# Two small projections moved onto one accumulator bank, their conversions reserved on VectorE, and score groups that carry a VectorE tile sent ahead

## The chip, the cores and the metric

The kernel runs on one core of one Trainium2 chip. The metric is the device time of one execution in microseconds, taken as the median of several runs.

## The reference

One transformer layer on 2048 rows of width 448. `h = x + Attention(LN(x))`, with 16 query heads of width 28 that share one key and one value head, and then `h2 = h + B(LN(h))`, where B adds a gated MLP for the 8 rows with the highest router score alone. Cut to what matters here:

```python
q = (x @ wq).reshape(B, S, H, Dh).transpose(0, 2, 1, 3); k = x @ wk; v = x @ wv
p = softmax(einsum("bhqd,bkd->bhqk", q, k) * Dh ** -0.5)
o = einsum("bhqk,bkd->bhqd", p, v)          # 16 heads, one K and one V
h = x + o.transpose(0, 2, 1, 3).reshape(B, S, H * Dh) @ wo
n = layernorm(h); r = n @ w_r; idx = argsort(-r)[:8]
h2 = h + n + scatter_add(idx, (silu(n[idx] @ w_gate) * (n[idx] @ w_up)) @ w_down * sigmoid(r[idx]))
```

Nearly all of the time goes into the 2048 x 2048 x 16 scores and their exponentials.

## The kernel before

**Blocks and slots.** The work goes over 16 blocks b of 128 query rows. A block has 64 score tiles: 16 groups of 128 keys by four lanes of 32 partitions, a lane holding four heads. A tile is 128 keys by 512 (four heads by 128 queries) and fills one of the eight PSUM banks. From block 1 on 16 of the 64 tiles go to VectorE and 48 to ScalarE. ScalarE's 48 are dealt into 17 slots, numbered 0 to 16: three tiles in most slots, two in the three slots that the tuple `TWO` names. A slot is one group of score matmuls on TensorE (`act_unit`, "a score group") and one exponential on ScalarE over its two or three banks (L760, the tile P).

**VectorE's tiles.** In every slot but the third of `TWO` (slot 11) the score group carries one matmul more, into the bank `VB`, for VectorE. `dve_tile` converts it to an integer form of the exponential (L785, the tile Y), which frees `VB` for the next score group. After every fourth tile `dve_batch` makes three shifted copies: two on VectorE (L794), one on GpSimd (L796). They are not started while the other engine holds the port that the planner models as shared (`port=True`). P and Y are multiplied with V on TensorE, four matmuls at a time (`pv_group`), all accumulating in the bank `ACC`. VectorE's tiles of a block begin four slots before the block (`LEAD`).

**Banks.** Score groups alternate between two halves, banks 0 to 2 in one slot and 3 to 5 in the next. A slot with two tiles leaves the third bank of its half free, and that bank is lent to a small projection ("misc"): in slot 2 the output projection of two blocks earlier (`out_proj`, four matmuls, then the residual sum `hbuf` on VectorE, L655), in slot 5 the query projection for two blocks later (`q_project`, 16 matmuls, then the conversion to `Q` on VectorE, L549). `misc(b, k)` gives the bank: 2 or 5, by whether the slot is even or odd. So the projections of slots 2 and 5 sit in different halves. The next score group of that half that has three tiles writes the lent bank, and so waits until the projection's result has been converted.

**The order on the engines.** Every engine runs its instructions in a fixed order. A planner in the kernel's Python (`_Graph.plan`) makes it beforehand from assumed durations. Three of its rules matter here:

- TensorE (`pe_choice`): score groups have `hold=AC`. Each has a last moment, a fixed lead before ScalarE comes free. Other work, P·V matmuls and projections, is put ahead of a score group if it ends before that moment.
- VectorE (`dve_choice`): operations marked `urgent` are reserved for. An operation that isn't urgent starts only if it ends within 150 ns of the moment at which the next urgent one becomes ready. Only the conversions of score tiles (`dve_tile`) are urgent.
- `fill` puts matmuls on zeros into TensorE's idle time.

`close_acc` copies a finished block's `ACC` to `Ot` (L805), and P·V matmuls of the next block wait for it. `post_block` divides it by the row sums by way of DRAM and GpSimd. After `hbuf` follow the statistics of the second layer norm (L657 to L671), the router's product `junk` (L690) and `r_col` (L693) on VectorE, and the two scaled copies on GpSimd (L682, L685).

Of the kernel before, what the change touches and what calls it, by code (L numbers as in the profile page):

```python
# [24 lines left out]
class _Graph:  # L25
# [5 lines left out]
    WINDOW = 3413.0  # L31
    FLOOR = 0.5
    SLIP = 150.0

    def __init__(self, sems, dma_sems, after=None):
        self.after = after
# [9 lines left out]
    def op(self, eng, fns, dur, reads=(), writes=(), prio=None, dma=False, name="", mode=None, pos=(0, 1, 2, 3),  # L46
           hold=None, deps=(), port=False, urgent=False, blk=None, kb=0):
        o = _Op()
        o.eng, o.dur, o.dma, o.name = eng, float(dur), dma, name
        o.mode, o.pos, o.hold, o.port, o.urgent, o.blk, o.kb = mode, pos, hold, port, urgent, blk, kb  # L50
        o.fns = list(fns) if isinstance(fns, (list, tuple)) else [fns]
        o.lat = 2700.0 if dma else self.LAT[eng]
        o.prio = 0.0 if self.after else (self.prio if prio is None else prio)
        o.idx = len(self.ops)
        o.deps = {}
        o.sig = False

        def need(p, sem):
            if p is not None and p is not o:
                o.deps[p.idx] = o.deps.get(p.idx, False) or sem  # L60

        for p in deps:
            need(p, not (p.eng == eng == PE) or p.dma)
        for k in reads:
            for p in self.last_w.get(k, ()):
                need(p, not (p.eng == eng == PE) or p.dma)
            if isinstance(k, tuple) and k[0] == "ps":
                for p in self.readers.get(k, ()):
                    if p.eng != eng:
                        need(p, True)  # L70
        for k in writes:
            for p in self.last_w.get(k, ()):
                need(p, (p.eng != eng) or (eng != PE) or p.dma)
            for p in self.readers.get(k, ()):
                need(p, p.eng != eng or p.dma or dma)
        if self.after and eng == PO and not dma:
            need(self.last_pool, True)
            self.last_pool = o
        for k in reads:
            self.readers.setdefault(k, []).append(o)  # L80
        for k in writes:
            self.last_w[k] = [o]
            self.readers[k] = []
        self.ops.append(o)
        return o
# [6 lines left out]
    def pe_choice(self, lst, free):  # L92
        t = free[PE]
        cand = [(self.pe_start(o, max(t, o.ready)), o) for o in lst]
        m = min(s for s, o in cand) + 1.0
        held = [(s, o, max(o.ready, free[o.hold] - self.LEAD_IN - 40.0)) for s, o in cand if o.hold]
        lim = min([l for s, o, l in held], default=1e12)
        now = [(o.prio, o.idx, s, o) for s, o, l in held if s <= m]
        if not now:
            now = [(o.prio, o.idx, s, o) for s, o in cand  # L100
                   if not o.hold and s <= m and s + o.dur + self.SWITCH <= lim + 1.0]
        if not now:
            p = min((s, o.prio, o.idx, o) for s, o, l in held if l <= lim + 1.0)
            return p[0], p[3]
        p = min(now)
        return p[2], p[3]
# [212 lines left out]
def _main(nc, G, sb, ps, psb, flag, scr, A_x, A_wq, A_wk, A_wv, A_wo, B_w_r, B_w_gate, B_w_up, B_w_down, out,  # L319
# [224 lines left out]
    def q_project(b, bank):  # L544
        pieces([mm(ps[:, bank, g * 128:(g + 1) * 128], wq_pad[0:CK, ch, g, :], xnT[0:CK, ch, b * 128:(b + 1) * 128],
                   ch == 0, ch == NCH - 1) for g in range(4) for ch in range(NCH)], 4, 56,
               reads=["wq_pad", ("xnT", b)], writes=[pk(bank)])
        q = b % NQ
        G.op(DV, lambda e: e.tensor_scalar(Q[:, q, :, :].rearrange("p g n -> p (g n)"), ps[:, bank, :], qone[:, 0:1],  # L549
                                           None, ALU.add), dvt(512),  # L550
             reads=[pk(bank), "qone"], writes=[("Q", q)], prio=G.prio - 900)

    GROUPS = [[0], [1], [2, 3], [4, 5], [6, 7], [8, 9], [10, 11], [12, 13], [14, 15]]

# [95 lines left out]
    def out_proj(b, bank):  # L650
        t, rb, hr = b, b % 2, b % 3
        tail = b == NB - 1
        pieces([mm(ps[:, bank, 0:D], On[:, rb, g * 128:(g + 1) * 128], wo_pad[:, g, :], g == 0, g == 3)
                for g in range(4)], 1, 189, reads=[("On", rb, 0), ("On", rb, 1), "wo_pad"], writes=[pk(bank)])
        G.op(DV, lambda e: e.tensor_tensor(hbuf[:, hr, :], ps[:, bank, 0:D], x_sb[:, t, :], ALU.add), dvt(D),  # L655
             reads=[pk(bank), ("x", t)], writes=[("h", hr)], prio=G.prio - 900)
        G.op(DV, lambda e: e.bn_stats(bn6[:, t, :], hbuf[:, hr, :]), dvt(D), reads=[("h", hr)], writes=[("bn6", t)])  # L657
        G.op(DV, lambda e: e.bn_aggr(mv[:, t, :], bn6[:, t, :]), 110, reads=[("bn6", t)], writes=[("mv", t)])
        G.op(DV, lambda e: e.tensor_scalar(st[:, t, 7:8], mv[:, t, 1:2], EPS, None, ALU.add), 70,
             reads=[("mv", t)], writes=[("st7", t)])  # L660
        if tail:
            G.op(AC, lambda e: e.activation(st[:, t, 7:8], st[:, t, 7:8], ACT.Ln), 200,
                 reads=[("st7", t)], writes=[("st7", t)])
            G.op(AC, lambda e: e.activation(st[:, t, 4:5], st[:, t, 7:8], ACT.Exp, scale=-0.5), 200,
                 reads=[("st7", t)], writes=[("st4", t)])
        else:
            G.op(PO, lambda e: e.tensor_tensor(st[:, t, 4:5], st[:, t, 7:8], nhalf[:, 0:1], ALU.pow), 600,
                 reads=[("st7", t), "nhalf"], writes=[("st4", t)])
        G.op(DV, lambda e: e.tensor_scalar(st[:, t, 5:6], st[:, t, 4:5], 1.0, None, ALU.add), 70,
             reads=[("st4", t)], writes=[("st5", t)])  # L670
        G.op(DV, lambda e: e.scalar_tensor_tensor(st[:, t, 6:7], mv[:, t, 0:1], -1.0, st[:, t, 4:5],  # L671
                                                  ALU.mult, ALU.mult), 80,
             reads=[("mv", t), ("st4", t)], writes=[("st6", t)])
        if tail:
            G.op(AC, lambda e: e.activation(xn[:, t, :], hbuf[:, hr, :], ACT.Identity, bias=st[:, t, 6:7],
                                            scale=st[:, t, 4:5]), 560,
                 reads=[("h", hr), ("st4", t), ("st6", t)], writes=[("xn", t)])
            G.op(AC, lambda e: e.activation(outf[:, t, :], hbuf[:, hr, :], ACT.Identity, bias=st[:, t, 6:7],
                                            scale=st[:, t, 5:6]), 560,
                 reads=[("h", hr), ("st5", t), ("st6", t)], writes=[("outf", t), ("x", t)])  # L680
        else:
            G.op(PO, lambda e: e.tensor_scalar(outf[:, t, :], hbuf[:, hr, :], st[:, t, 5:6], st[:, t, 6:7],  # L682
                                               ALU.mult, ALU.add), 800,
                 reads=[("h", hr), ("st5", t), ("st6", t)], writes=[("outf", t), ("x", t)])
            G.op(PO, lambda e: e.tensor_scalar(xn[:, t, :], hbuf[:, hr, :], st[:, t, 4:5], st[:, t, 6:7],  # L685
                                               ALU.mult, ALU.add), 800,
                 reads=[("h", hr), ("st4", t), ("st6", t)], writes=[("xn", t)])
        if not tail:
            evs.append(dma(out_v[:, t, :], outf[:, t, :], [("out", t)], reads=[("outf", t)], prio=G.prio + 30))
        G.op(DV, lambda e: e.scalar_tensor_tensor(junk[:, :], hbuf[:, hr, :], st[:, t, 4:5], w_rb[:, :],  # L690
                                                  ALU.mult, ALU.mult, accum_out=st[:, t, 2:3]), 700,
             reads=[("h", hr), ("st4", t), "w_rb"], writes=["junk", ("st2", t)], port=True)
        G.op(DV, lambda e: e.scalar_tensor_tensor(r_col[:, t:t + 1], st[:, t, 6:7], sw[:, 0:1], st[:, t, 2:3],  # L693
                                                  ALU.mult, ALU.add), 80,
             reads=[("st6", t), "sw", ("st2", t)], writes=[("r", t)], port=True)

    NVB = [0] + [4] * (NB - 1)
    LEAD = 4
    TWO = (2, 5, 11)
    TWO_LAST = (2, 7, 11)  # L700
    LAG = 4
    slots = []
# [43 lines left out]
    def act_unit(n):  # L746
# [7 lines left out]
        if v:  # L754
# [1 line left out]
            reads += [("Q", v[0] % NQ), ("K", v[1])]  # L756
            writes.append(pk(VB))
            pos.append(vi)
        sops.append(G.op(PE, fns, 216, mode="S", pos=pos, hold=AC, reads=reads, writes=writes, prio=t - 30))
        G.op(AC, lambda e: e.activation(P[:, s0:s0 + w, :], ps[:, b0:b0 + w, :], ACT.Exp,  # L760
                                        bias=-(ZERO + SHIFT) * OCT, scale=OCT), w * 427 + 50,
             reads=[pk(b0 + k) for k in range(w)], writes=[("P", s0 + k) for k in range(w)], prio=t - 30)
# [205 lines left out]
    t = NT - 1  # L968
# [182 lines left out]
```

## Time and profile before

| | |
|---|---|
| median of 3 runs | 438.6 us (437.02 to 438.82) |
| the profiled execution | 440.31 us, span 438.4 us |
| TensorE busy | 343.5 us (78%) |
| VectorE busy | 337.7 us (77%) |
| ScalarE busy | 371.7 us (85%), of which 358.7 us are the 281 exponentials of L760 |
| GpSimd busy | 186.1 us (42%) |
| mean granted TensorE clock | 0.986; 1.00 from block 1 to block 15, half in one stretch of some 10 us after the last block |

No engine is full: the busiest has 15% of the span idle. Two warnings for the reading. A matmul's end is modelled, so TensorE's busy share is no measure of how full it is. And an exponential that follows another overlaps its predecessor's end, so that the time lost between two is read from the distance of their ends and not from the idle time alone.

### The profile page before, as it was taken

To read this page: it belongs to the slowest core of one execution; us is meant where nothing else is said; L and a number is where in the kernel's file an instruction comes from. 1 tells how busy PE (TensorE), PEld (TensorE's weight loads), DVE (VectorE), ACT (ScalarE), POOL (GpSimd) and SP (SyncE) were. 2 spreads that over 40 slices of the span, in tenths; PEclk is the share of its full clock that TensorE was granted. 3 is DMA by queue.
4 is the path that set the end of the run, shared out by engine and by line. 5 is a ranking of instruction groups with operands and counts; after the bars stand their busy time and mean duration, and the time that the engine had idled before them with its cause. 6 is when DMAs were issued, how large, how long until landed. Compare 5 with 4: busy or idle time off the path is not lost.

```text
span 438.4 us, 9042 instructions
## 1 busy us (share of the span) xinstructions
PE 343.5 (78%) x3718; PEld 131.1 (30%) x3718; DVE 337.7 (77%) x708; ACT 371.7 (85%) x311; POOL 186.1 (42%) x200
## 2 busy tenths in 40 slices
PE   3899777877777778778787777787878777786994
PEld 2445321312222322222232222222223221222673
DVE  6965686979797978888897978787979787976333
ACT  4768799999989899999999998989898989995130
POOL 5332134362536363544535363635454545363001
PEclk9999999999999999999999999999999999999599
DMA  8991000010101010101000000000010101000000
GB/s 211 216 243 29 0 4 26 3 37 2 37 3 37 2 37 2 38 2 35 2 26 14 16 22 9 32 4 34 4 37 3 37 3 37 3 12 12 1 2 20
DMA packets 15782, 14.18 MB, mean 32 GB/s; under 512 B 6061, under 2 KB 12981, under 8 KB 15733
## 3 DMA queue, kind: packets, MB, share of 16 engines
q1 hardware_dynamic: 15701, 13.51, 11.5%
q8 instruction: 32, 0.52, 0.5%
q14 instruction: 17, 0.14, 0.1%
q0 software_dynamic: 32, 0.01, 0.0%
HBM read 11.42 MB, written 2.09 MB: 31 GB/s over the span
## 4 chain that ended last, share of the span: by engine, by line
DVE 46%; PE 34%; ACT 13%; issue 4%; DMA 1%; POOL 0%; SPq 0%; POOLq 0%
PE ps L436 33%; DVE Y L785 24%; ACT P L760 13%; DVE Y L794 8%; DVE Ot L805 2%; DVE Q L549 2%; PE ps L439 2%; DVE junk L690 2%; DVE bn L657 2%; DVE hbuf L655 2%; DVE r_col L693 2%; DMA wq_sb<-in_A_wq_dram 1%; DVE xnT L594 1%; DVE K L604 1%; DVE Y L1016 0%
## 5 line engine op out<-in xcount | busy, mean ns | idle before, releaser
L760 ACT ACTIVATE P<-ps 128x1536 bf16<-128x1536 f32 (+2 forms) x281 | 358.7, 1405 | 31.8 <-PE ps L436 29.3
L785 DVE TENSOR_SCALAR Y<-ps 128x512 int16<-128x512 f32 x240 | 165.1, 688 | 58.2 <-PE ps L436 58.1
L796 POOL TENSOR_TENSOR Y<-Y,step 128x1024 int32<-128x1024 int32 x60 | 113.4, 1890 | 149.3 <-DVE Y L794 90.3
L436 PE MATMUL ps<-Q,K 32*128 32x512 bf16 x1024 | 113.3, 389 | 61.2 <-DVE Y L785 44.7
L436 PE MATMUL ps<-Y,Vs 128*32 128x512 bf16 x960 | 86.8, 385 | 16.6 <-DVE Ot L805 11.3
L794 DVE TENSOR_SCALAR Y<-Y 128x2048 int16<-128x2048 int16 x120 | 82.1, 684 | 0.1
L436 PEld LDWEIGHTS ps<-Q,K 32*128 32x128 bf16 x1024 | 33.1, 91 | 159.8 <-ACT P L760 128.0
L436 PE MATMUL ps<-P,Vs 128*32 128x512 bf16 x784 | 76.2, 392 | 0.3 <-ACT P L760 0.3
L436 PEld LDWEIGHTS ps<-Y,Vs 128*32 128x32 bf16 x960 | 22.1, 93 | 59.1 <-issue 19.6
L436 PE MATMUL ps<-zero 128*32 128x512 bf16 x115 | 34.9, 386 | 0.0
L682 POOL TENSOR_SCALAR x_sb<-hbuf,st 128x448 bf16<-128x448 f32 x15 | 15.1, 1005 | 33.5 <-DVE st L671 33.5
L436 PEld LDWEIGHTS ps<-P,Vs 128*32 128x32 bf16 x784 | 18.9, 93 | 33.5 <-issue 30.1
L641 POOL TENSOR_TENSOR On<-Ot,Rb 128x256 bf16<-128x256 f32 x30 | 21.2, 724 | 1.5 <-DMA Rb<-l_scr 1.5
L436 PE MATMUL ps<-xnT,wq_pad 112*128 112x128 bf16 x256 | 20.9, 232 | 0.6 <-DVE mv L562 0.6
L617 POOL TENSOR_SCALAR Vs<-Vf 128x64 bf16<-128x64 f32 (+1 forms) x36 | 8.9, 248 | 24.9 <-DVE Vf L614 23.2
L436 PEld LDWEIGHTS ps<-xnT,wq_pad 112*128 112x128 bf16 x256 | 15.8, 103 | 7.6 <-issue 7.5
L1041 POOL DMA_INDIRECT out_dram<-Y,idxu x1 | 1.1, 1116 | 35.7 <-issue 35.7
L436 PE MATMUL ps<-wo_pad,On 128*128 128x448 bf16 x64 | 15.7, 363 | 0.4 <-POOL On L641 0.4
L549 DVE TENSOR_SCALAR Q<-ps,qone 128x512 bf16<-128x512 f32 x16 | 11.9, 743 | 3.3 <-PE ps L436 3.3
L439 PE MATMUL ps<-ident,xn 128*112 128x128 bf16 x68 | 8.5, 291 | 6.3 <-DVE xn L572 6.3
L436 PEld LDWEIGHTS ps<-zero 128*32 128x32 bf16 x115 | 10.9, 97 | 7.9 <-issue 1.3
L690 DVE SCALAR_TENSOR_TENSOR junk<-hbuf,st,w_rb 128x448 f32<-128x448 f32 x16 | 11.7, 733 | 0.0
(159 smaller groups left out, 226.9 us busy)
## 6 DMA issues: line engine op xcount, KB each, us to landing
Rb<-l_scr SPq DMA_DIRECT2D x14, 256.0 KB
out_dram<-x_sb SPq DMA_DIRECT2D x15, 112.0 KB, 1.7
wg_sb<-in_B_w_gate_dram SPq DMA_DIRECT2D x1, 1568.0 KB, 15.0
wu_sb<-in_B_w_up_dram SPq DMA_DIRECT2D x1, 1568.0 KB, 21.7
wd_sb<-in_B_w_down_dram SPq DMA_DIRECT2D x1, 1568.0 KB, 25.1
x_sb<-in_A_x_dram SPq DMA_DIRECT2D x3, 448.0 KB, 5.7
wq_sb<-in_A_wq_dram SPq DMA_DIRECT2D x2, 196.0 KB, 3.0
wo_pad<-in_A_wo_dram SPq DMA_DIRECT2D x4, 98.0 KB
```

Source lines behind the costliest of these rows:

```text
L436: return lambda e: e.matmul(o, lhsT=l, rhs=r, start=start, stop=stop)
L439: return lambda e: e.transpose(o, i, ident[0:p, 0:p])
L549: G.op(DV, lambda e: e.tensor_scalar(Q[:, q, :, :].rearrange("p g n -> p (g n)"), ps[:, bank, :], qone[:, 0:1], None, ALU.add), dvt(512), ...
L617: G.op(PO, lambda e, v=v: e.tensor_scalar(Vs[:, v, t0:t0 + n, :], Vf[:, t0:t0 + n, :], VC[v], 1.0, ALU.mult, ALU.mult), 150 + 32 * n * 1.5 ...
L641: G.op(PO, lambda e, c=c: e.tensor_tensor(On[:, rb, c], Ot[:, rb, c], Rb[:, rb, c], ALU.mult), 750, reads=[("Ot", rb), ("Rb", rb)], writes ...
L655: G.op(DV, lambda e: e.tensor_tensor(hbuf[:, hr, :], ps[:, bank, 0:D], x_sb[:, t, :], ALU.add), dvt(D), reads=[pk(bank), ("x", t)], writes ...
L682: G.op(PO, lambda e: e.tensor_scalar(outf[:, t, :], hbuf[:, hr, :], st[:, t, 5:6], st[:, t, 6:7], ALU.mult, ALU.add), 800, reads=[("h", hr ...
L690: G.op(DV, lambda e: e.scalar_tensor_tensor(junk[:, :], hbuf[:, hr, :], st[:, t, 4:5], w_rb[:, :], ALU.mult, ALU.mult, accum_out=st[:, t, ...
L760: G.op(AC, lambda e: e.activation(P[:, s0:s0 + w, :], ps[:, b0:b0 + w, :], ACT.Exp, bias=-(ZERO + SHIFT) * OCT, scale=OCT), w * 427 + 50, ...
L785: G.op(DV, lambda e: e.tensor_scalar(Y[:, y, 0, q, :].bitcast(I16), ps[:, VB, :], 0.0, 32639.0 - STEP[3], ALU.max, ALU.min), dvt(512), rea ...
L794: done = [G.op(DV, lambda e, c=c: e.tensor_single_scalar(y[c].bitcast(I16), y[0].bitcast(I16), STEP[c], ALU.add), 600, reads=r, writes=[(" ...
L796: G.op(PO, lambda e: e.tensor_tensor(y[3].bitcast(I32), y[0].bitcast(I32), step3[:, 0:1].broadcast_to([128, 1024]), ALU.add), 2050, reads= ...
```

## The change

- The second entry of `TWO` goes from 5 to 4: the slots with two tiles are 2, 4 and 11. Slots 2 and 4 are of one half, so both projections use the same bank, one after the other, and slot 4's score group doesn't write it. The next score group that does is that of slot 6. The query projection is queued one slot earlier. The last block keeps its own tuple `TWO_LAST`, (2, 7, 11).
- The conversions `Q` (from block 3 on) and `hbuf` become urgent in the planner.
- A score group that carries a VectorE tile is urgent for `pe_choice`: its last moment is at most 100 ns (`EARLY`) after it is ready.
- A GpSimd operation that writes what an earlier GpSimd operation read now waits for it by a semaphore.

```diff
+    EARLY = 100.0
...
             for p in self.readers.get(k, ()):
-                need(p, p.eng != eng or p.dma or dma)
+                need(p, p.eng != eng or p.dma or dma or eng == PO)
...
-        held = [(s, o, max(o.ready, free[o.hold] - self.LEAD_IN - 40.0)) for s, o in cand if o.hold]
+        held = [(s, o, max(o.ready, min(free[o.hold] - self.LEAD_IN - 40.0, o.ready + self.EARLY
+                                        if o.urgent else 1e12))) for s, o in cand if o.hold]
...
         # q_project: the conversion to Q
-             reads=[pk(bank), "qone"], writes=[("Q", q)], prio=G.prio - 900)
+             reads=[pk(bank), "qone"], writes=[("Q", q)], prio=G.prio - 900, urgent=b > 2)
...
         # out_proj: hbuf
-             reads=[pk(bank), ("x", t)], writes=[("h", hr)], prio=G.prio - 900)
+             reads=[pk(bank), ("x", t)], writes=[("h", hr)], prio=G.prio - 900, urgent=True)
...
-    TWO = (2, 5, 11)
+    TWO = (2, 4, 11)
...
-        sops.append(G.op(PE, fns, 216, mode="S", pos=pos, hold=AC, reads=reads, writes=writes, prio=t - 30))
+        sops.append(G.op(PE, fns, 216, mode="S", pos=pos, hold=AC, reads=reads, writes=writes, prio=t - 30,
+                         urgent=bool(v)))
```

## Rows read from the trace of the kernel before

**Rows 1.** Busy times by stretch: length; PE, PEld, DVE, ACT, POOL; PEclk; DMA share, GB/s

```profile
106.64:336.92 230.28, 183.01 (x2030) 60.39 (x2030) 193.37 (x361) 218.73 (x171) 111.94 (x90) 1.00 0.06 19
```

**Rows 2.** Who waited for whom: us in total, times, longest

```profile
ACT P L760 <- PE ps L436: 29.3, 32, 3.0
...
PE ps L436 <- DVE hbuf L655: 2.9, 13, 0.2
```

**Rows 3.** Chain that ended last: start, us, what; conversion to Q

```profile
106.64 0.66 DVE Q L549
...
336.92 0.66 DVE Q L549
```

**Rows 4.** Timeline of ScalarE, slots 1 to 6 and 13: start, us, instruction

```profile
191.89 2.48 ACT L760 ACTIVATE P<-ps 128x1536 bf16<-128x1536 f32 x2
...
194.45 1.45 ACT L760 ACTIVATE P<-ps 128x1536 bf16<-128x1536 f32 x1
...
196.86 1.45 ACT L760 ACTIVATE P<-ps 128x1536 bf16<-128x1536 f32 x1 [0.96 <-PE ps L436]
...
198.21 1.02 ACT L760 ACTIVATE P<-ps 128x1024 bf16<-128x1024 f32 x1
...
199.34 1.45 ACT L760 ACTIVATE P<-ps 128x1536 bf16<-128x1536 f32 x1
...
208.25 1.52 ACT L760 ACTIVATE P<-ps 128x1536 bf16<-128x1536 f32 x1
```

**Rows 5.** Timeline of TensorE, slots 2 to 4, and slot 12

```profile
192.49 0.39 PE L436 MATMUL ps<-Q,K 32*128 32x512 bf16 x3
192.81 0.93 PE L436 MATMUL ps<-wo_pad,On 128*128 128x448 bf16 x4
193.67 0.40 PE L436 MATMUL ps<-Y,Vs 128*32 128x512 bf16 x4
194.00 0.40 PE L436 MATMUL ps<-Q,K 32*128 32x512 bf16 x4
...
196.42 0.40 PE L436 MATMUL ps<-Q,K 32*128 32x512 bf16 x4 [0.22 <-DVE hbuf L655]
196.75 0.84 PE L436 MATMUL ps<-xnT,wq_pad 112*128 112x128 bf16 x12
...
206.22 0.40 PE L436 MATMUL ps<-Q,K 32*128 32x512 bf16 x4
```

**Rows 6.** Timeline of VectorE, slots 2 to 5

```profile
192.93 0.69 DVE L785 TENSOR_SCALAR Y<-ps 128x512 int16<-128x512 f32 x1
193.53 0.68 DVE L794 TENSOR_SCALAR Y<-Y 128x2048 int16<-128x2048 int16 x1
194.45 0.69 DVE L785 TENSOR_SCALAR Y<-ps 128x512 int16<-128x512 f32 x1 [0.23 <-PE ps L436]
195.06 0.68 DVE L805 COPY Ot<-ps 128x512 f32<-128x512 f32 x1
195.66 0.61 DVE L655 TENSOR_TENSOR hbuf<-ps,x_sb 128x448 f32<-128x448 f32 x1
```

**Rows 7.** Timeline of VectorE, slots 11 to 14

```profile
205.79 0.68 DVE L690 SCALAR_TENSOR_TENSOR junk<-hbuf,st,w_rb 128x448 f32<-128x448 f32 x1
...
206.51 0.55 DVE L693 SCALAR_TENSOR_TENSOR r_col<-st,sw 128x1 f32<-128x1 f32 x1
206.98 0.68 DVE L785 TENSOR_SCALAR Y<-ps 128x512 int16<-128x512 f32 x1
208.25 0.69 DVE L785 TENSOR_SCALAR Y<-ps 128x512 int16<-128x512 f32 x1 [0.59 <-PE ps L436]
209.54 0.69 DVE L785 TENSOR_SCALAR Y<-ps 128x512 int16<-128x512 f32 x1 [0.59 <-PE ps L436]
```

**Rows 8.** Groups of the page: busy, mean ns, idle before

```profile
L794 DVE TENSOR_SCALAR Y<-Y 128x2048 int16<-128x2048 int16 x120 | 82.1, 684 | 0.1
```

**Rows 9.** Timeline of VectorE, block 15, while GpSimd ran L682 and L685

```profile
388.31 0.85 DVE L794 TENSOR_SCALAR Y<-Y 128x2048 int16<-128x2048 int16 x1
```

## The prediction

> **What bounds the kernel now.** I read the waits first. ScalarE's exponentials wait for TensorE 29.3 us in all [rows 2]; that is the largest idle time of the busiest engine, so I looked for where in a block it lies. The chain that ended last shows the conversion to Q at the same place of each block: from 106.64 to 336.92 are ten blocks [rows 3], 23.03 us each. In that stretch the granted clock is 1.00 and no engine is full (ScalarE 218.7 of 230.3 us) [rows 1], so it is a matter of waits.
>
> A block's floor on ScalarE comes from distances of ends (start plus length). The two-bank exponential of slot 5 ends 0.92 after its predecessor (198.31 to 199.23) [rows 4]. Slot 6's ends at 200.79 and slot 13's at 208.25 + 1.52 = 209.77 [rows 4]; of these 8.98 us slot 11 has 0.92, and the six over three banks 1.343 each. 14 x 1.343 + 3 x 0.92 = 21.56. The block takes 23.03: 1.47 us are lost in each. The ends of slots 2, 3, 4, 5 and 6 are 194.37, 195.90, 198.31, 199.23, 200.79 [rows 4]: slot 3 loses 1.53 - 1.34 = 0.19, slot 4 1.07, slot 6 0.22, together 1.48.
>
> Slot 4's cause stands in its row: the score group at 196.42 waited for `hbuf` [rows 5], because slot 4 writes the bank that the output projection borrowed in slot 2. The projection's matmuls had ended at 193.74 [rows 5], but VectorE took an L794 copy at 193.53, then Y, then Ot, and `hbuf` only at 195.66 to 196.27 [rows 6]. The waits name `hbuf` 13 times [rows 2]: blocks 3 to 15 each have this stall. (The 0.2 us given there is only TensorE's idle time; what the end of the exponential lost is 1.07.) Slot 3's cause: the VB bank came free at 193.62, when Y ended [rows 6], but TensorE put a Y·V group at 193.67 ahead, and the scores went at 194.00 [rows 5]. Slot 6 is the step behind the late slot 4.
>
> There is a second loop with hardly any slack, through the single VB bank: score matmuls, Y, next score matmuls. Where nothing disturbs it Y follows Y after 1.285 us (208.25 to 209.54) [rows 7], of which 0.45 are from scores to Y (194.00 to 194.45) [rows 5, 6]. ScalarE needs 1.343 for three banks, but 0.92 in a two-bank slot, so around slots 2 to 5 the VB loop is the slower one.
>
> A sum over both checks this. From the scores of slot 12 to those of slot 4 are nine steps of the loop, 11.57; the late Y of slot 12 adds 0.31 (below), slot 3 0.23 and slot 4 1.13 (1.51 and 2.42 between the scores [rows 5], less 1.285). From slot 4's scores to the end of its exponential 1.89 (196.42 to 198.31), then 0.92, 1.56 and four times 1.343 to slot 10's end, which is 200.79 + 5.37 = 206.16, and 0.06 from there to slot 12's scores at 206.22 [rows 5]: 9.80. Together 23.04, against 23.03.
>
> **The change, part by part.** *Slot 4 no longer writes the lent bank.* Its wait for `hbuf` goes whatever VectorE does: -1.07, and with it -0.22 in slot 6. *Urgent score groups*: the Y·V group goes behind slot 3's scores: -0.19. That alone, if all else stayed, would be 13 x 0.19 = 2.5 us. P·V groups slide back behind the scores. TensorE has room for them: a group of four holds it for 0.33 (193.67 to 194.00) [rows 5], and a block's 17 score groups and 28 P·V groups make 14.9, with some 1.8 for the two projections 16.7 of 23.
>
> With all of it gone the block would be at ScalarE's 21.56. What the VB loop then allows: slot 12's scores to slot 5's are ten steps, 12.85; from there ScalarE leads again: 0.45 + 1.45 for slot 5's exponential (three banks now), five of 1.343 to slot 10's end, 0.06 to slot 12's scores: 8.68. Together 21.53. So the two loops are all but level, and every delay of a Y between slots 12 and 5 lengthens the block, less 0.03. The delays:
>
> *`hbuf` reserved on VectorE.* It becomes ready in the middle of a loop step: the projection ends 1.25 after slot 2's scores began (192.49 to 193.74) [rows 5], `hbuf` can start at about 1.30 and takes 0.61 [rows 6], until 1.91. The Y of slot 3 would be due at 1.285 + 0.45 = 1.735. It is 0.18 late. The L794 copy that stood at 193.53 is refused there and moves to a later gap: the VectorE has 230.3 - 193.4 = 36.9 us idle in ten blocks [rows 1], 3.7 a block, and the gaps in front of Y are 0.59 [rows 7], each large enough for one. Bounds: 0 if it falls into a gap, 0.61 if Y waits for all of it.
>
> *The Q conversion reserved.* Its matmuls need `hbuf` done (1.91) and take about 0.9 (estimated from 0.84 for twelve, end included [rows 5]); some go before slot 4's scores, some behind. Its turn then comes after slot 4's Y, in a gap that it fills (0.66 [rows 3] against 0.675, the loop's 1.285 less 0.61 of Y from 194.45 to 195.06 [rows 6]). Cost 0; bounds 0 and 0.66.
>
> *`junk` and `r_col`.* They stay, 205.79 to 206.98 = 1.19 us [rows 7]; slot 12's Y, due 0.45 after the scores at 206.22 [rows 5], came at 206.98: 0.31 late. They follow `hbuf`, so their place moves; I keep 0.31. Bounds 0 and 0.52 (1.19 less a gap of 0.675).
>
> *Semaphore waits on GpSimd.* Operations that rewrite what GpSimd read occur in the setup alone; in a block its writes go to tiles that other engines read. GpSimd is busy 111.9 of 230.3 us [rows 1], which hides them: 0, and if a hit came in a block, one wait of a few tenths off the path.
>
> Sum: 0.18 + 0 + 0.31 = 0.49 of delay, less 0.03 of slack: the block takes 21.56 + 0.46 = 22.02, 1.01 less than 23.03. Thirteen blocks have the stall: 13.1 us. The profiled execution (440.31, span 438.4) is 1.7 above the median; from it this gives 427.2, from the median 425.5. I predict 426. In general, with d the delay per block, the time is 438.6 - 13 x (1.50 - d), and not below 438.6 - 13 x 1.47 = 419.5.
>
> **The rivals.** *ScalarE sets the pace (d under 0.3: 420 to 423).* For it: old gaps of 0.59 stand empty. Against: `hbuf` and the router's operations have lengths that don't fit the gap.
>
> *The conversions cost Y whole turns (d 0.8 to 1.33: 429 to 436).* If Q's last matmuls fall behind slot 5's scores, its conversion comes after slot 5's Y and ends at 0.45 + 0.61 + 0.66 + 0.1 = 1.82 after those scores; slot 6, the next that writes the shared bank, was due at 1.285: +0.54, d = 1.03, 432.5. For it: the matmuls can't start before 1.91, and slot 4's scores, due at 2 x 1.285 + 0.18 = 2.75, now go ahead of what is left of them. Against: what is left then has a whole step before slot 5's.
>
> *No measurable change (d 1.33 to 1.67).* The same wait in slot 6, and `hbuf` holding slot 3's Y for its full 0.61 instead of 0.18: d = 1.03 + 0.43 = 1.46, 438.1. The stall of slot 4 would have become one of slot 6.
>
> *Slower: VectorE and GpSimd collide.* The planner lays L794 and GpSimd's work apart by assumed durations; in a denser block the real ones overlap. In block 15 an L794 copy under GpSimd's scaling took 0.85 [rows 9] against a mean of 0.684 over all 120 [rows 8]: +0.17. With d = 0.49 it takes (1.67 - 0.49) / 0.17, seven of a block's eight copies, to be slower by over 0.5%; all eight give d = 1.85, 443. Against it: the mean of 0.684 says that nearly none collides now. The Trainium skill (GPSIMD Engine Reference, section Key points) states that GpSimd shares its SBUF interfaces with VectorE and contends with VectorE instructions in a two-port mode; the trace agrees with this 0.85, and by that rule every overlap would be paid, which is what this rival assumes.
>
> **How the numbers follow.** About 0.5%, 2.2 us, can be told from no change. Forecast (d 0.3 to 0.8, 423 to 429.5) 0.45; ScalarE's pace 0.15; whole turns 0.20; no change 0.10; slower 0.10. Faster is 0.45 + 0.15 + 0.20 = 0.80. For 8 in 10 the range goes from 420 (next to nothing lies under the floor) to 437, which leaves out the slower case and most of the no-change one.
>
> **What would show it.** Right: the distance from one Q conversion to its match a block later is near 22.0; slot 4's scores wait for Y and not for `hbuf`; slot 3's scores start when Y ends; `hbuf` stands directly ahead of slot 3's Y; no exponential of slots 3 to 6 ends over 0.5 late. Wrong: slot 6's scores wait for Q (second and third rival), or L794's mean length is well above 0.684 (fourth), or the order that the planner makes differs from block to block. The prediction falls if the planner, whose assumed loop differs from the measured 1.285, packs more than one operation into VectorE's gaps of 0.675.

## The result and the profile after

The changed kernel takes 426.81 us (median of 4 runs, 422.86 to 430.47) against 438.71 us (437.02 to 440.9): a ratio of 0.970, interval 0.960 to 0.979. Executions over 1.5% longer than the fastest of their kernel count in the medians of this document and not in the ratios, so that the two need not match. The profiled execution took 428.56 us, its span is 426.8 us.

First the page of the changed kernel, and its busy times in one stretch in which both of its longer blocks lie (columns as in [rows 1]):

```profile
PE 339.0 (79%) x3709; PEld 129.4 (30%) x3709; DVE 342.9 (80%) x708; ACT 370.2 (87%) x311; POOL 195.6 (46%) x200
...
L797 DVE TENSOR_SCALAR Y<-Y 128x2048 int16<-128x2048 int16 x120 | 85.3, 712 | 0.1
```

```profile
95.00:314.00 219.00, 176.59 (x2006) 58.25 (x2006) 195.34 (x358) 215.60 (x169) 116.57 (x90) 1.00 0.06 20
```

The busy times hardly change and the waits do. The waits of the changed kernel, as in [rows 2]:

```profile
ACT P L763 <- PE ps L438: 17.7, 31, 3.0
...
PEld ps L438 <- DVE hbuf L657: 5.8, 13, 0.7
```

ScalarE's wait for TensorE falls from 29.3 to 17.7 us. `hbuf` is still waited for 13 times, but now by the query projection's first weights, which want its bank, and no longer by scores.

Now one block (block 7, slots 2 to 6) on TensorE, to be laid beside [rows 5]:

```profile
184.16 0.39 PE L438 MATMUL ps<-Q,K 32*128 32x512 bf16 x3
184.48 0.93 PE L438 MATMUL ps<-wo_pad,On 128*128 128x448 bf16 x4
185.43 0.40 PE L438 MATMUL ps<-Q,K 32*128 32x512 bf16 x4
185.76 0.62 PE L438 MATMUL ps<-P,Vs 128*32 128x512 bf16 x8
186.31 0.40 PE L438 MATMUL ps<-xnT,wq_pad 112*128 112x128 bf16 x4
186.82 0.39 PE L438 MATMUL ps<-Q,K 32*128 32x512 bf16 x3
187.15 0.84 PE L438 MATMUL ps<-xnT,wq_pad 112*128 112x128 bf16 x12
188.09 0.40 PE L438 MATMUL ps<-Q,K 32*128 32x512 bf16 x4
...
189.52 0.40 PE L438 MATMUL ps<-Q,K 32*128 32x512 bf16 x4 [0.27 <-DVE Y L788]
```

and on VectorE, beside [rows 6] (the last row is the next block's conversion to Q):

```profile
184.59 0.69 DVE L788 TENSOR_SCALAR Y<-ps 128x512 int16<-128x512 f32 x1
185.45 0.62 DVE L657 TENSOR_TENSOR hbuf<-ps,x_sb 128x448 f32<-128x448 f32 x1 [0.17 <-PE ps L438]
185.99 0.68 DVE L788 TENSOR_SCALAR Y<-ps 128x512 int16<-128x512 f32 x1
186.59 0.68 DVE L808 COPY Ot<-ps 128x512 f32<-128x512 f32 x1
187.26 0.69 DVE L788 TENSOR_SCALAR Y<-ps 128x512 int16<-128x512 f32 x1
188.03 0.75 DVE L551 TENSOR_SCALAR Q<-ps,qone 128x512 bf16<-128x512 f32 x1
188.70 0.68 DVE L788 TENSOR_SCALAR Y<-ps 128x512 int16<-128x512 f32 x1
...
209.96 0.75 DVE L551 TENSOR_SCALAR Q<-ps,qone 128x512 bf16<-128x512 f32 x1
```

Slot 3's scores follow the projection at once (185.43) with no Y·V group between. `hbuf` stands directly ahead of slot 3's Y, which was due at 185.43 + 0.45 = 185.88 and starts at 185.99. Slot 4's scores, at 186.82, wait for nothing but the Y that ended at 186.67. The distance from one Q conversion to the next is 209.96 - 188.03 = 21.93 us, against 23.03 in [rows 3].

The end of each exponential gives what is left per regular block: 0.29 us in slot 5 and 0.09 in slot 6, instead of 0.19, 1.07 and 0.22 in slots 3, 4 and 6. Blocks 9 and 12 are longer: 22.96 us. In block 9 a VectorE row of slot 1 is out of line, and GpSimd's rows beside it say why. VectorE:

```profile
226.51 1.79 DVE L797 TENSOR_SCALAR Y<-Y 128x2048 int16<-128x2048 int16 x1
```

GpSimd:

```profile
223.94 1.97 POOL L643 TENSOR_TENSOR On<-Ot,Rb 128x256 bf16<-128x256 f32 x2 [1.28 <-DMA Rb<-l_scr]
225.86 1.89 POOL L799 TENSOR_TENSOR Y<-Y,step 128x1024 int32<-128x1024 int32 x1
```

The broadcast `Rb` landed late, `On` waited 1.28 us for it, the copy on GpSimd came later than planned and ran until 227.75, and VectorE's copy, which should take 0.68, ended 0.55 after that. That is the collision that the fourth rival was made of. Ahead of block 12, the other long one, `On` waited again, and nowhere else in the blocks did it wait over 0.1 us. GpSimd:

```profile
291.03 1.70 POOL L643 TENSOR_TENSOR On<-Ot,Rb 128x256 bf16<-128x256 f32 x2 [1.54 <-DMA Rb<-l_scr]
```

### The profile page after: what moved, and what is told of

Same layout as the page of the kernel before. It is cut to its first block, busy times and chain, and to the rows that moved or that the text cites. A ratio compares the mean times of both kernels' runs of the same rounds, so it can differ in the third digit from the quotient of the medians.

```text
span 426.8 us, 9032 instructions
## 1 busy us (share of the span) xinstructions
PE 339.0 (79%) x3709; PEld 129.4 (30%) x3709; DVE 342.9 (80%) x708; ACT 370.2 (87%) x311; POOL 195.6 (46%) x200
## 4 chain that ended last, share of the span: by engine, by line
PE 42%; DVE 30%; ACT 21%; issue 5%; DMA 1%; POOL 0%; SPq 0%; POOLq 0%
PE ps L438 40%; ACT P L763 21%; DVE Y L788 15%; DVE Y L797 4%; DVE Q L551 2%; DVE junk L692 2%; PE ps L441 1%; DVE r_col L695 1%; DVE xnT L596 1%; DVE K L606 1%; DMA wq_sb<-in_A_wq_dram 1%; DVE Ot L808 0%; DVE Y L1019 0%; DVE hbuf L657 0%; DVE mv L660 0%
## 5 line engine op out<-in xcount | busy, mean ns | idle before, releaser
L763 ACT ACTIVATE P<-ps 128x1536 bf16<-128x1536 f32 (+2 forms) x281 | 357.4, 1416 | 17.8 <-PE ps L438 17.7
L788 DVE TENSOR_SCALAR Y<-ps 128x512 int16<-128x512 f32 x240 | 165.5, 689 | 38.0 <-PE ps L438 37.2
L438 PE MATMUL ps<-Y,Vs 128*32 128x512 bf16 x960 | 84.4, 383 | 5.1 <-DVE Y L797 2.4
L438 PEld LDWEIGHTS ps<-Q,K 32*128 32x128 bf16 x1024 | 34.3, 91 | 170.3 <-ACT P L763 135.4
L797 DVE TENSOR_SCALAR Y<-Y 128x2048 int16<-128x2048 int16 x120 | 85.3, 712 | 0.1
L438 PE MATMUL ps<-P,Vs 128*32 128x512 bf16 x784 | 75.2, 388 | 0.1
L438 PEld LDWEIGHTS ps<-Y,Vs 128*32 128x32 bf16 x960 | 22.2, 94 | 35.5 <-issue 16.3
L643 POOL TENSOR_TENSOR On<-Ot,Rb 128x256 bf16<-128x256 f32 x30 | 22.9, 784 | 2.9 <-DMA Rb<-l_scr 2.8
L687 POOL TENSOR_SCALAR xn<-hbuf,st 128x448 bf16<-128x448 f32 x15 | 17.4, 1158 | 0.0
L657 DVE TENSOR_TENSOR hbuf<-ps,x_sb 128x448 f32<-128x448 f32 x16 | 10.0, 624 | 4.3 <-PE ps L438 4.3
L441 PE MATMUL ps<-ident,xn 128*112 128x128 bf16 x68 | 7.6, 269 | 6.4 <-DVE xn L574 6.4
```

What stands on the lines that cost most here:

```text
L438: return lambda e: e.matmul(o, lhsT=l, rhs=r, start=start, stop=stop)
L441: return lambda e: e.transpose(o, i, ident[0:p, 0:p])
L643: G.op(PO, lambda e, c=c: e.tensor_tensor(On[:, rb, c], Ot[:, rb, c], Rb[:, rb, c], ALU.mult), 750, reads=[("Ot", rb), ("Rb", rb)], writes ...
L788: G.op(DV, lambda e: e.tensor_scalar(Y[:, y, 0, q, :].bitcast(I16), ps[:, VB, :], 0.0, 32639.0 - STEP[3], ALU.max, ALU.min), dvt(512), rea ...
L797: done = [G.op(DV, lambda e, c=c: e.tensor_single_scalar(y[c].bitcast(I16), y[0].bitcast(I16), STEP[c], ALU.add), 600, reads=r, writes=[(" ...
```

## The experiments

A block's length below is the distance between the ends of exponentials. Every ratio is to the kernel before on the same chip.

**The parts one by one.** The tuple alone, in the kernel before:

```diff
-    TWO = (2, 5, 11)
+    TWO = (2, 4, 11)
```

> The kernel before with the tuple of two-bank slots changed to (2, 4, 11) and nothing else. My theory (a block takes 21.53 us plus the delay of score tiles between slots 12 and 5): slot 4 no longer waits for hbuf, but hbuf is still converted late (after the L794 copy, Y and Ot, about 3.8 us behind slot 2's scores), so the query projection starts late on the same bank and slot 6 waits for Q instead: a block of 22.6 to 23.0 us, 433 to 438 us in all. Rival, that moving the slot alone removes the stall: 22.0 us a block, 426 us.

437.6 us, ratio 0.995 (0.991 to 0.999). Blocks alternate, 24.29 and 21.73 us. Nearly the whole difference is one stall of 2.33 us in slot 6 of every second block. TensorE and then VectorE in block 5:

```profile
146.68 1.07 PE L436 MATMUL ps<-xnT,wq_pad 112*128 112x128 bf16 x16
149.04 0.40 PE L436 MATMUL ps<-Q,K 32*128 32x512 bf16 x4 [1.30 <-DVE mv L658]
```

```profile
145.14 0.61 DVE L655 TENSOR_TENSOR hbuf<-ps,x_sb 128x448 f32<-128x448 f32 x1
145.82 0.69 DVE L785 TENSOR_SCALAR Y<-ps 128x512 int16<-128x512 f32 x1
146.43 1.28 DVE L794 TENSOR_SCALAR Y<-Y 128x2048 int16<-128x2048 int16 x2
147.63 0.62 DVE L657 BATCH_NORM_STATS2 bn<-hbuf 128x6 f32<-128x448 f32 x1
148.16 0.73 DVE L549 TENSOR_SCALAR Q<-ps,qone 128x512 bf16<-128x512 f32 x1
```

The conversion to Q ends at 148.89 and slot 6's scores follow at 149.04. (The row names the statistics, which end at 148.98; what these scores need is the bank that Q's conversion frees.) As expected, the stall of slot 4 has become one of slot 6.

The early score groups alone:

```diff
+        held = ... min(free[o.hold] - self.LEAD_IN - 40.0, o.ready + self.EARLY if o.urgent else 1e12) ...
+        sops.append(G.op(PE, fns, 216, mode="S", ..., urgent=bool(v)))
```

> Of the change only the early score groups: the two-bank slots are (2, 5, 11) and no conversion is reserved. As I priced it: slot 3's 0.19 us per block comes back, hbuf stays late, slot 4 still waits: 22.8 us a block, 436 us. Rival, after the run without the early groups cost 28 us more than the changed kernel: they are worth much by themselves, 430 us or less.

434.06 us, ratio 0.986 (0.978 to 0.993). Slot 3's loss is gone as expected, but slot 4's falls too, from 1.07 to between 0.36 and 0.96: blocks of 22.13 to 22.73 us. The expectation (22.8, 436) was too small a gain, the rival (430) too large.

The reservation alone:

```diff
-             ... writes=[("Q", q)], prio=G.prio - 900)
+             ... writes=[("Q", q)], prio=G.prio - 900, urgent=b > 2)
-             ... writes=[("h", hr)], prio=G.prio - 900)
+             ... writes=[("h", hr)], prio=G.prio - 900, urgent=True)
```

> Of the change only the reservation of the Q and hbuf conversions. Loop theory: hbuf ends 1.9 us behind slot 2's scores, slot 4 doesn't wait: 22.2 us a block, 428 us. Rival, that a score group queued behind a Y.V group waits with it for GpSimd's copy, as in the run without the early groups: one such stall of 2.5 us in most blocks, 24 us a block, over 445 us.

439.93 us, ratio 0.999 (0.995 to 1.003). Neither the 428 us of the loop theory nor the rival's 445 came. Again there are two sorts of block: 22.20, as the loop theory had it, and 23.77. The long ones have an L794 copy of 1.80 us in slot 1, under GpSimd's copy (165.76 to 167.65):

```profile
166.40 1.80 DVE L794 TENSOR_SCALAR Y<-Y 128x2048 int16<-128x2048 int16 x1
```

**The parts taken away one by one.** Without the early groups (`urgent=bool(v)` removed):

> The changed kernel without the early score groups (none marked urgent). My theory: slot 3's scores go behind a Y.V group again, 0.2 us per block back: 22.1 us a block, 13 x 0.2 = 2.6 us more than the changed kernel. Rival, that the score order is what brings the gain: 22.6 us a block or more, over 434 us.

455.22 us, ratio 1.036 (1.030 to 1.041); 24.14 us a block, 2.58 of loss in slot 5 (block 14 takes 29.67, with 6.87 lost in that slot). My expectation of 22.1 is far off. VectorE in block 6:

```profile
168.87 1.28 DVE L796 TENSOR_SCALAR Y<-Y 128x2048 int16<-128x2048 int16 x2
170.31 0.75 DVE L551 TENSOR_SCALAR Q<-ps,qone 128x512 bf16<-128x512 f32 x1 [0.15 <-PE ps L438]
170.98 0.62 DVE L659 BATCH_NORM_STATS2 bn<-hbuf 128x6 f32<-128x448 f32 x1
...
171.94 0.69 DVE L787 TENSOR_SCALAR Y<-ps 128x512 int16<-128x512 f32 x1
```

Slot 4's scores are at 169.10 there, so its Y was due at 169.55; it is placed behind two copies, Q and the statistics, and in the program it waits for GpSimd, whose copy ends at 171.91. The copies have been put so far back that one of the three Y buffers isn't free. The rival's number is nearer, but not its mechanism: it is VectorE's tile that waits, and the score group behind it.

Without the reservation (both `urgent` flags of the conversions removed):

> The changed kernel without the reservation of the Q and hbuf conversions on VectorE. My theory: hbuf waits behind a copy again and slot 6 waits for Q: 22.4 to 22.8 us a block, 431 to 436 us. Rival, that the reservation is worth nothing once both projections share the bank: 21.9 us a block, 427 us.

442.59 us, ratio 1.006 (1.002 to 1.011): blocks of 24.15 and 22.17 in turn, with the same 2.33 us in slot 6 as with the tuple alone. The theory names the right place; the size was 0.5 us a block too small.

With the slots at (2, 5, 11) and all the rest:

> The changed kernel with the two-bank slots back at (2, 5, 11). My theory: with hbuf reserved it is done 1.9 us behind slot 2's scores, and slot 4's are due at 2.57, so slot 4 doesn't wait even where it writes the lent bank: 22.0 us a block, 426 to 428 us, the same as the changed kernel; the move of the slot is worth next to nothing. Rival, that the shared bank is what removes the stall: 22.8 us or more a block, over 435 us.

465.5 us, ratio 1.058 (1.050 to 1.065); blocks 2 to 13 take 22.2 to 26.2 us and block 15 32.3. I had expected no difference. From block 5 to block 13 slot 13 loses 1.36, and the granted clock falls to half in the blocks. A stretch of that and what stands at slot 13 of block 8, VectorE and then GpSimd:

```profile
213.50:223.00 9.50, 8.85 (x56) 1.77 (x57) 5.67 (x12) 8.30 (x7) 3.31 (x3) 0.50 0.04 13
```

```profile
236.37 1.85 DVE L673 SCALAR_TENSOR_TENSOR st<-mv,st 128x1 f32<-128x1 f32 x1
238.14 0.68 DVE L788 TENSOR_SCALAR Y<-ps 128x512 int16<-128x512 f32 x1
```

```profile
236.30 1.89 POOL L799 TENSOR_TENSOR Y<-Y,step 128x1024 int32<-128x1024 int32 x1
```

`st6` (L673), one number per partition, takes 1.85 us in place of 0.15: it starts 0.07 after GpSimd's copy and ends with it. Y and with it the scores stand behind it. The planner does not count this operation as a user of the shared port.

**Is it the collision?** First by telling the planner (`port=True` on that operation):

> The changed kernel with the slots back at (2, 5, 11), as in the run of 465.5 us, but with the small product st6 (L673, two SBUF inputs, 1.84 us instead of 0.15 under GpSimd's copy) entered in the planner as a user of the shared port. Theory that the collision makes that run slow: the stall of 1.36 us in slot 13 is gone, the granted clock doesn't fall in the blocks, under 440 us. Rival, that the slots' banks are what makes it slow: 455 us or more.

466.23 us, ratio 1.061 (1.053 to 1.068). L673 has a median of 1.847 us as before. Neither theory is touched: the flag moves nothing, every engine has the same order as without it. (That the planner, by its assumed times, sees no overlap there is my reading and isn't shown.) Then by taking the second SBUF input away, in `st6` and in `r_col`, which had the same form:

```diff
-        G.op(DV, lambda e: e.scalar_tensor_tensor(st[:, t, 6:7], mv[:, t, 0:1], -1.0, st[:, t, 4:5], ...
+        G.op(DV, lambda e: e.tensor_scalar(st[:, t, 6:7], mv[:, t, 0:1], st[:, t, 4:5], -1.0, ...
-        G.op(DV, lambda e: e.scalar_tensor_tensor(r_col[:, t:t + 1], st[:, t, 6:7], sw[:, 0:1], st[:, t, 2:3], ...
+        G.op(DV, lambda e: e.tensor_scalar(r_col[:, t:t + 1], st[:, t, 6:7], sw[:, 0:1], st[:, t, 2:3], ...
```

> The changed kernel with the slots back at (2, 5, 11), the run of 465.5 us, with the same two operations rewritten. Theory that a two-input operation of 128 numbers waited for GpSimd's copy there: L673 is back at 0.15 us, slot 13's stall of 1.36 us is gone, 9 blocks x 1.36 = 12 us or more less, and more if the clock then stays up; under 450 us. Rival: the banks of slots 2 and 5 make it slow, 460 us or more.

436.49 us, ratio 0.993 (0.989 to 0.997), 29 us less than the same order with the old form. (Two products were rewritten at once, and the clock stayed up with it: of the 29 us some 12 are slot 13's, the rest isn't told apart.) In block 8 the operation again starts 0.06 behind GpSimd's copy. GpSimd, then VectorE:

```profile
227.08 1.89 POOL L799 TENSOR_TENSOR Y<-Y,step 128x1024 int32<-128x1024 int32 x1
```

```profile
227.14 0.20 DVE L673 TENSOR_SCALAR st<-mv,st 128x1 f32<-128x1 f32 x1
```

It takes 0.20 us. Slot 13's stall is gone, the clock stays at 1.00 from block 1 to block 14, and blocks 5 to 13 take 22.2 us but for two. What is left over the changed kernel is 0.6 us in slot 7 of each block and 6.8 us in slot 5 of block 15. Slot 7's scores write the bank that the query projection borrows in slot 5, and wait for the conversion to Q: in block 8 it runs from 219.85 to 220.59 and they follow at 220.74. Against the changed kernel with the same two products rewritten (21.82 a block, below) the old place of the slot costs 0.4 us a block. So the expectation, that its move is worth next to nothing, was too low, and the rival's 22.8 too high. The Trainium skill (GPSIMD Engine Reference, section Key points) says that GpSimd shares its SBUF interfaces with VectorE, with contention for VectorE instructions that have two SBUF inputs or run in a two-port mode. The pair of rows agrees for two inputs, and shows that the whole of GpSimd's operation is waited for.

**The same rewriting in the changed kernel**, with the order of every engine unchanged:

> The changed kernel with st6 (L673) and r_col (L695) written as operations with one SBUF tensor input and per-partition scalars; the order on every engine is the same. Theory that r_col's 0.55 us is a wait for GpSimd's scaling, which ends at the same moment, over the shared port: r_col 0.2 us or less, slot 12's Y no longer 0.28 late, slot 5's stall of 0.29 gone, a block 21.6 us instead of 21.93, 12 x 0.3 = 3.6 us less than the changed kernel, about 423 us. Rival, that r_col's length is its own: no change.

428.28 us, ratio 0.968 (0.963 to 0.974). `r_col` falls from 0.55 to 0.27, so its length had been a wait; but a regular block is 21.82, 0.11 less and not 0.3. VectorE then comes to the next copies earlier and finds GpSimd in the way there:

```profile
177.82 0.28 DVE L695 TENSOR_SCALAR r_col<-st,sw 128x1 f32<-128x1 f32 x1
178.01 0.68 DVE L788 TENSOR_SCALAR Y<-ps 128x512 int16<-128x512 f32 x1
...
179.89 0.88 DVE L797 TENSOR_SCALAR Y<-Y 128x2048 int16<-128x2048 int16 x1
```

GpSimd's copy runs until 180.22 there. L797's mean rises to 748 ns. Three blocks, 7, 9 and 12, take 22.57 to 22.85; they are the ones ahead of which `On` waited for `Rb` (1.04, 1.22 and 1.03 us), so they are of this execution and not of the rewriting. In all no gain can be told: the ratio is 0.968, as in the changed kernel's repeat below. In the kernel before:

> The kernel before with the same two operations rewritten. By the sum over the loops (9 steps, plus 0.31 for the late Y of slot 12, 0.23, 1.13 and 9.80) a block loses the 0.31: 22.73 instead of 23.03 us, 4 us less, 434.7 us. Rival, that slot 4's wait takes it up: 23.03.

437.59 us, ratio 0.995 (0.991 to 0.999); 22.81 us a block. Of the 0.31 that the sum gave to the late Y 0.22 comes back in a block. Over twelve blocks that is 2.6 us; the medians differ by 0.9, with a scatter of several us.

**Moving GpSimd's `On`** (the assumed time of the transfer `Rb`, `.lat`, from 3900 to 6500 ns):

> The changed kernel with the planner's assumed time for the broadcast of the reciprocal sums (Rb) raised from 3.9 to 6.5 us, so that GpSimd's On is put later in its order. Theory that the two long blocks (22.96 us) come from an L797 copy that waits while GpSimd's copy, held up by a late On, uses the shared port: no L797 over 0.8 us, no block over 22.1 us between 4 and 13, 2 us less in the profile. Rival, that the long copy has another cause: it is there again.

470.56 us, ratio 1.070 (1.062 to 1.077). The planner made another order, in which blocks 4, 7, 10 and 13 take 32 to 33 us, with VectorE and GpSimd in lockstep. VectorE in block 4:

```profile
131.29 5.30 DVE L797 TENSOR_SCALAR Y<-Y 128x2048 int16<-128x2048 int16 x5
136.51 2.31 DVE L692 SCALAR_TENSOR_TENSOR junk<-hbuf,st,w_rb 128x448 f32<-128x448 f32 x1
...
138.91 1.67 DVE L695 SCALAR_TENSOR_TENSOR r_col<-st,sw 128x1 f32<-128x1 f32 x1
```

The other blocks take 21.9 to 22.0. It doesn't test what it was made for. Of the 8.6 us that slot 9 loses there, some 5 are collisions (five copies take 5.30 in place of 3.4, `junk` 2.31 in place of 0.68, `r_col` 1.67 in place of 0.20); the rest is that all of these stand ahead of one Y.

**The changed kernel once more:**

> The changed kernel once more, on the same chip. Theory that the long blocks come from a late transfer that lets GpSimd's copy fall on an L797 copy: which blocks are long differs from the first profile, or there is none; the others are 21.93 us again.

426.07 us, ratio 0.968 (0.963 to 0.973). Blocks 3 to 13 take 21.93, blocks 9 and 12 among them; only block 14 is longer (22.25), with an L797 copy of 1.18. `On` waited for `Rb` just ahead of that block too, and of no other. GpSimd:

```profile
335.90 1.41 POOL L643 TENSOR_TENSOR On<-Ot,Rb 128x256 bf16<-128x256 f32 x2 [0.51 <-DMA Rb<-l_scr]
```

So the long blocks belong to one execution, and the 21.93 to both. In all three executions of this order every longer block comes behind such a wait: 22.02 and 22.25 us behind 0.30 and 0.51, 22.57 to 22.96 behind 1.03 to 1.54. That bears the theory out, though no run moved `Rb` by itself.

## Why the prediction was right, and where not

**The stalls removed.** Right: slot 4's wait for `hbuf`, slot 3's Y·V group and slot 6's echo were the 1.48 us, and all three went.

**The sum of delays.** `hbuf` ahead of slot 3's Y: 0.18 predicted, 0.11 measured (185.88 to 185.99). Q: 0 predicted, 0.16 measured. Its gap is 0.675 wide and it takes 0.67, but its last matmuls ran until 187.99, so it began at 188.03 and Y, due at 188.54, came at 188.70; it delays slot 6 and makes the 0.09 there. `r_col`: 0.31 predicted, 0.28 measured, in these rows of VectorE, slots 11 and 12:

```profile
197.10 0.55 DVE L695 SCALAR_TENSOR_TENSOR r_col<-st,sw 128x1 f32<-128x1 f32 x1
197.57 0.68 DVE L788 TENSOR_SCALAR Y<-ps 128x512 int16<-128x512 f32 x1
```

The scores were at 196.84, so Y was due at 197.29. TensorE, slot 12 a block earlier and here:

```profile
174.91 0.39 PE L438 MATMUL ps<-Q,K 32*128 32x512 bf16 x4
...
196.84 0.39 PE L438 MATMUL ps<-Q,K 32*128 32x512 bf16 x4
```

With 0.11 and 0.28 between slots 12 and 5 the two loops give 21.53 + 0.39 = 21.92, with 21.93 measured and 22.02 predicted. Taken apart at slot 5's scores (188.09), the first part took 13.18, where the sum has 12.85 + 0.39 = 13.24, and the second 8.75, where it has 8.68, since slot 6's 0.09 stands outside it. So the loop sum holds to 0.1 us, and that it meets the block to 0.01 is luck.

**The thirteen blocks.** 13.1 us predicted. Blocks 3 to 14 gave 11.0 (276.17 to 265.17 us from the end of block 2), of which the two long blocks cost 2.05: 13.05 without them. Block 15 gave 0.15 and not 1.0: its slot 4 lost its stall, but slots 12 and 15 together lost 1.06 more. The 0.95 of slot 15 is a stall of the old kind: its scores wait for the `hbuf` of another output projection. TensorE:

```profile
381.50 0.39 PE L438 MATMUL ps<-Q,K 32*128 32x512 bf16 x3 [0.40 <-DVE hbuf L657]
```

Blocks 1 and 2, which I had left out, gave 1.2.

**What no step foresaw, and what cancelled.** Block 0 ended 2.96 us earlier with the same order of instructions on TensorE, because TensorE ran faster sooner. (The trace's first record of the granted clock, 1.00, begins at 28.2 us here and at 37.2 in the kernel before, and none stands ahead of it; so the level there isn't shown, though the views print 1.00.) Its transposes, eight at a time, take 1.10 us until 36 us in the kernel before; in the changed kernel:

```profile
24.46 1.10 PE L441 MATMUL ps<-ident,xn 128*112 128x128 bf16 x8
29.02 0.65 PE L441 MATMUL ps<-ident,xn 128*112 128x128 bf16 x8
```

In the repeat of the changed kernel they take 1.10 at 29.43 and block 0 is as long as before, so this is not the change. And the end, from the last exponential on, took 41.4 us instead of 37.8: the granted clock was at its lower level from 386.6 to 403.7 us, 17.1 us, against 10.2 us in the kernel before (405.8 to 416.0). Whether the change brings the longer stretch isn't settled; other executions of the changed kernel have a mean clock of 0.981, against 0.973 here, and spans of 421.1 and 423.2. In the repeat the stretch was 17.0 us (388.7 to 405.7), in the changed kernel with the rewritten products 13.6, and in the kernel before with them 10.2: this leans towards the change and does not prove it. That 426.0 lies 0.8 from 426.81 is in part luck: these two errors of three to four us have opposite signs.

**A term mis-sized: the early score groups.** I priced them at slot 3's 0.19, 2.5 us in all. Alone they were worth 1.4% (0.986), since `hbuf` came earlier too (1.07 to 1.67 us behind its projection, against 1.92), and taken out of the whole they cost 28 us. The same holds for the other parts: the tuple alone gives 0.5%, the reservation alone nothing, and no pair without the third is faster than the kernel before (1.036, 1.006, 1.058). I argued the parts as independent edits of one schedule. Each of them makes the planner lay out all engines anew, and what a pair loses is not the part left out but a new wait: Q's conversion in slot 6, a Y buffer that isn't free, a two-input operation under GpSimd's copy.

**The rival of collisions** had a chance of 0.10 and a price of 0.17 a hit. Its price was far too low: the 0.17 came from a copy (388.31) that met only the last 0.30 us of GpSimd's L682, which ended at 388.61. A hit costs up to the whole of GpSimd's operation, 1.1 us for an L797 copy and 1.7 us for `st6`. It happened in blocks 9 and 12 of the first profile and three times in its block 15 (the mean of the copies went from 684 to 712 ns, the sign that the prediction had named), in half of the blocks of one part alone, and decided the slowest pair.

**Open**: why block 15 loses 0.6 us in each of its last slots before and after (there the scores start only when the exponential ahead of them has ended, 383.45 behind 383.39), and how much of the tail's clock is the change's. Neither was tried.

## What to carry to other kernels

Where two loops of nearly equal length share engines (here ScalarE's 21.56 and the single-bank loop's 21.53 us a block), write both as sums, and price an edit by what it delays on the longer one: this gave the block to 0.1 us. Don't add up the parts of a change to a planned order; run the pairs. And look for the operations that slip under another engine's long one: in one order of this kernel two small products of one number per partition cost more than the projections that the change was about.

## What the runs showed of the hardware

- A VectorE operation with two SBUF inputs of 128 x 1 waits for a GpSimd operation that began just ahead of it until that ends: 1.85 us instead of 0.15. With one input and a per-partition scalar it takes 0.20 in the same place.
- An int16 copy of 128 x 2048 on VectorE, 0.68 us by itself, takes 0.88 to 1.80 us under GpSimd's int32 copy, and 2.38 us in the worst row. In each of the three rows shown here it ends 0.55 us after GpSimd's operation (228.30 and 227.75, 168.20 and 167.65, 180.77 and 180.22).
- The moment at which TensorE's matmuls become faster at the start varied between 22 and 37 us over the executions, with block 0 between 48.6 and 53.5 us, the same order of TensorE's instructions in it. The first record of the granted clock, 1.00, begins with the faster matmuls (28.2 and 37.2 us in the first two profiles); the level ahead of it is not on record.
